# Phases and their trigonometry for two steps at a time in an S4 + SwiGLU block

## The chip, the cores and the metric

The kernel runs on one core of one Trainium2 chip. The core has a matrix engine (TensorE, PE), a vector engine (VectorE, DVE), an activation engine (ScalarE, ACT) and a general engine (GpSimd, POOL). Each works through its own list of instructions in order and waits on semaphores for what the others make. Loads and stores go through queues: most are issued by SyncE (SP), some by ACT and POOL. Weights and tables lie in the on-chip memory SBUF; PE writes its results to a small memory, PSUM, which DVE and ACT read. The metric is the device time of one execution in microseconds (us); less is better. The figure compared is the median of three executions.

## The reference, cut to what matters

```python
x = A_u                                              # (1, L=2048, D=640)
sa, ca, ga, sb, cb, gb = six rows of silu(c) @ w_mod
h = layernorm(x) * (1 + ca) + sa
x = x + ga * S4(h)
h = layernorm(x) * (1 + cb) + sb
x = x + gb * ((silu(h @ w1) * (h @ w3)) @ w2)        # F = 1728
# S4, for every channel d with N = 128 states n:
dt = exp(log_dt); logdA = dt * (A_re + i A_im); dB = dt * (B_re + i B_im)
K[d, l] = Re sum_n C[d, n] * dB[d, n] * exp(logdA[d, n] * l)      # l = 0 .. 2047
y = causal convolution of u with K over l (by FFT of length 2L) + u * Dskip
```

What matters here is K. For every channel and state the kernel needs exp of a real exponent times the cosine and sine of a phase, for 2048 values of l. It splits l = 64 a + b (a of 32, b of 64), so a channel needs only 32 + 64 complex factors per state, and the sum over the states becomes a matrix product of the "a" factors with the "b" factors.

## The kernel before, in words

The 640 channels are worked through in 40 **steps** of 16 channels (SD = 16); 8 steps are one chunk of 128 channels (SPC = 8). The states lie on the 128 partitions. A step s goes through these parts, each a short function with a two-letter name:

- PH (`phases`, lines 477-483, POOL): the phase in 32-bit integers, where a full turn is 2^32 and wraps by itself. One multiply of 16 channels x 64 factors (`thi` times the table `iota`), and one add of `phi` for the 32 "a" factors.
- AB, CO, SI (`absph`, `cosine`, `sine`, lines 485-496, ACT): the absolute value of the phase, from it the cosine, and the sine in place.
- PA, PQ (`exponents`, lines 441-454, PE): the real exponents, as a product of the transposed parameters `lx` with a selection table (`r2` for the 64 "b" factors, `r1` for the 32 "a" factors); each is two matmuls over all 128 rows, of 512 and of 256 columns. XA, XQ (`fast`, `slow`, ACT): exp of them, into the table A.
- E1, E2, A1, A2 (lines 504-518, DVE): exp times cosine into E, exp times sine in place into A. All four read both inputs from SBUF.
- kg (`kgen`, PE): 64 small products that give K of the step; K (`k1evac`, DVE, lines 537 and 538); pt (`k_stage1`, PE, line 548) and uk (`k_out`, ACT): the first stage of the transform of K.

A second group of parts does the convolution of an earlier chunk in 40 units of its own: st (`stage2`, PE, line 579, with the load of its table s2 on SP), kc (`k_copy`, ACT, a copy of half the result to SBUF), T (`products`, DVE, 596 and 597), Y (`sums`, DVE, 603 and 604), iv (`inverse1`, PE, 621, with its load of i1) and zt (`z_store`, ACT and a store).

From step 10 on, the parts follow an order written out by hand, the string `ROUND` (lines 829-835): one **round** takes four steps and four convolution units, and is repeated ten times (the first and last only in part). "E1+2" is part E1 of step 4*round + 2. In the rounds PE, ACT, DVE and POOL keep exactly this order (`keep_in_program_order`). Convolution units run with a lag of ten steps. Rounds 2 to 6 carry four extra pieces (LS, LP, LC, LO) that finish the modulation rows. The exponents of all steps share one pair of PSUM banks, so PA, XA, PQ, XQ of a step and PA of the next form a chain; st, kc, T, Y and the next st share another pair in the same way.

Before the rounds a prologue loads parameters, makes `lx` (`polar`, lines 232-292: the transposes of the tile `lt` at 282, a copy on ACT and a subtraction on DVE), the tables `r2` and `r1` (743, 747), the first layer norm and the transform of u. There a scheduler of the language sets the order. Behind the rounds come the last convolution units and then the SwiGLU part (all helper-recorded, so its lines read L103), which the change does not touch.

Lines that the prediction names: phases are lines 481 and 482 on POOL; AB, CO and SI are L136 `cs<-ph`, `cs<-cs` and `ph<-ph`, the exps L136 `A<-pa`; the copies kc, uk and zt are L139; E1, E2, A1, A2 are 506, 509, 513, 517.

## Time and profile before

| | us |
|---|---|
| median of 3 executions (997.47, 1000.23, 1000.56) | 1000.23 |
| the profiled execution, its own time | 991.63 |
| its span, first to last instruction | 989.8 |
| prologue, until the rounds are full (0 to 149) | 149 |
| full rounds (149 to 349) | 200 |
| last round, last convolution units (349 to 404) | 55 |
| SwiGLU part (404 to 990) | 586 |

How to read the profile: an answer of the timeline has a start, a duration, the engine, the line and the operation, then what it writes `<-` what it reads; in square brackets stands how long the engine had been idle and what released it. "xN" merges N instructions. Durations of neighbours on one engine overlap a little, since the next instruction starts while the last drains; the distance from start to start is then the cost, and the prediction calls it the cadence. A view by stretches gives the busy time of each engine within a piece of the span; the granted clock is the share of full speed that PE was allowed. A row of a group has the number of instructions, then their busy time and the mean of one in ns.

### The profile page before, as it was taken

The page shows a single profiled execution, that of the slowest core. Times are in us where ns is not written, and L with a number is a line of the kernel's source. Part 1 is how long each engine was busy: PE and PEld are TensorE (multiplying, and loading weights), DVE is VectorE, ACT ScalarE, POOL GpSimd, SP SyncE. Part 2 cuts the span into 40 slices and gives each one's busy share as a digit, 9 for nine tenths or more (in the row PEclk, how much of TensorE's full clock was granted, in tenths as well). Part 3 has the DMA queues.
Part 4 walks back from the last instruction along what each step waited for, and adds up shares of the span by engine and source line. Part 5 has one row for each costly group of instructions (what it writes and reads, how often), then busy time and mean ns, then how long its engine had stood idle before and what let it go on. Part 6 is the DMA issues. An engine that isn't in the chain of part 4 may idle for free.

```text
span 989.8 us, 20130 instructions
## 1 busy us (share of the span) xinstructions
PE 904.1 (91%) x7964; PEld 679.0 (69%) x7964; DVE 734.0 (74%) x1224; ACT 539.9 (55%) x792; POOL 348.5 (35%) x330
## 2 busy tenths in 40 slices
PE   5777779999999889789999999989899999999998
PEld 3334456666666666567888887676678888888786
DVE  5888978998888876677566675777696666676765
ACT  4759688899999943355333333453653333333332
POOL 1733344444444600323222232355342222314441
PEclk9865779999999999999999999999999999999999
DMA  9572285666676679691211104978231111123351
GB/s 265 206 253 93 108 196 140 174 180 175 195 220 152 176 199 291 201 246 53 67 54 54 54 28 140 256 221 261 80 120 54 54 55 57 56 87 94 96 205 72
DMA packets 103570, 140.72 MB, mean 142 GB/s; under 512 B 20564, under 2 KB 62676, under 8 KB 103476
## 3 DMA queue, kind: packets, MB, share of 16 engines
q1 hardware_dynamic: 92692, 113.60, 39.7%
q10 hardware_dynamic: 8480, 18.09, 6.2%
q0 software_dynamic: 2304, 7.74, 2.3%
q8 instruction: 63, 1.03, 0.4%
q14 instruction: 31, 0.25, 0.1%
HBM read 107.94 MB, written 31.46 MB: 141 GB/s over the span
## 4 chain that ended last, share of the span: by engine, by line
PE 42%; DVE 5%; DMA 3%; ACT 2%; POOL 2%; issue 2%; SPq 1%; DVEq 0%; ACTq 0%; POOLq 0%
PE ps L103 42%; DMA A<-zs 2%; DVE ul L103 1%; DVE T L103 1%; DVE xm L103 1%; DMA rw<-in_w_dram 1%; DVE gl L103 1%; ACT s L103 1%; ACT gh L103 1%; DMA xm<-in_x_dram 1%; SPq L103 1%; DVE s L103 1%; POOL s L103 0%; POOL S L103 0%; DVE h L103 0%
## 5 line engine op out<-in xcount | busy, mean ns | idle before, releaser
L103 DVE TENSOR_TENSOR s<-ps,s 128x512 f32<-128x512 f32 x138 | 94.6, 686 | 76.6 <-PE ps L103 76.0
L481 POOL TENSOR_TENSOR ph<-thi,iota 128x1024 int32<-128x1024 int32 x40 | 85.3, 2133 | 161.5 <-DVE A L517 101.1
L103 DVE TENSOR_TENSOR gl<-rw,gh 128x640 fp32r<-128x640 f32 x87 | 84.6, 972 | 62.6 <-ACT gh L103 62.5
L103 ACT CAST gh<-rw 128x640 fp32r<-128x640 f32 x87 | 63.2, 726 | 115.2 <-PE ps L103 77.2
L103 POOL TENSOR_TENSOR rw<-rw,gbr 128x512 f32<-128x512 f32 x56 | 82.2, 1476 | 105.0 <-DMA rw<-in_w_dram 87.2
L103 POOL TENSOR_TENSOR S<-rw 128x256 f32<-128x256 f32 x46 | 35.0, 764 | 176.4 <-DVE S0l L103 157.4
L579 PE MATMUL p<-uk,s 128*64 128x256 f32 x640 | 79.2, 390 | 15.8 <-PE pa L447 5.8
L103 PE MATMUL ps<-gh,uh 128*128 128x512 f32 x224 | 89.3, 398 | 0.0
L103 PE MATMUL ps<-gl,uh 128*128 128x512 f32 x224 | 89.2, 398 | 0.0
L103 PE MATMUL ps<-xA,gh 128*128 128x512 f32 x280 | 87.8, 392 | 0.7 <-ACT xA L103 0.4
L103 PE MATMUL ps<-gh,ul 128*128 128x512 f32 x208 | 82.7, 398 | 0.0
L136 ACT ACTIVATE A<-pa 128x1024 f32<-128x1024 f32 (+1 forms) x80 | 64.3, 813 | 27.1 <-PE pa L447 25.0
L579 PEld LDWEIGHTS p<-uk,s 128*64 128x64 f32 x640 | 45.9, 138 | 39.5 <-PE pa L447 8.4
L447 PE MATMUL pa<-r,lx 128*128 128x512 f32 (+1 forms) x160 | 52.1, 415 | 10.7 <-ACT A L136 5.6
L103 PEld LDWEIGHTS ps<-xA,gh 128*128 128x128 f32 x280 | 52.2, 188 | 13.7 <-ACT xA L103 1.0
L103 PE MATMUL ps<-xA,gl 128*128 128x512 f32 x140 | 54.6, 390 | 0.2 <-DVE gl L103 0.2
L513 DVE TENSOR_TENSOR A<-A,ph 128x1024 f32<-128x1024 f32 x40 | 52.6, 1315 | 0.0
L506 DVE TENSOR_TENSOR E<-A,cs 128x1024 f32<-128x1024 f32 x40 | 50.2, 1254 | 0.7 <-ACT cs L136 0.7
L103 PEld LDWEIGHTS ps<-gl,uh 128*128 128x128 f32 x224 | 43.1, 193 | 9.4
L447 PEld LDWEIGHTS pa<-r,lx 128*128 128x128 f32 x160 | 25.8, 203 | 34.5 <-ACT A L136 18.2
L103 PEld LDWEIGHTS ps<-gh,uh 128*128 128x128 f32 x224 | 43.2, 193 | 9.1
L530 PE MATMUL pk<-E 128*32 128x64 f32 x1280 | 46.4, 236 | 3.4 <-DVE E L509 3.4
(229 smaller groups left out, 2280.2 us busy)
## 6 DMA issues: line engine op xcount, KB each, us to landing
rw<-in_w_dram ACTq DMA_DIRECT2D x44, 320.0 KB
us<-u SPq DMA_DIRECT2D x16, 640.0 KB
s<-in_s_dram SPq DMA_DIRECT2D x40, 256.0 KB
i<-in_i_dram SPq DMA_DIRECT2D x40, 256.0 KB
rw<-in_wg_dram SPq DMA_DIRECT2D x31, 320.0 KB
rw<-in_wu_dram SPq DMA_DIRECT2D x28, 320.0 KB
uk<-us SPq DMA_DIRECT2D x32, 256.0 KB
zs<-zt SPq DMA_DIRECT2D x32, 256.0 KB
```

The source lines that it names most:

```text
L103: ins = fn(*args, **kw)
L136: return tc.keep_in_program_order(S.activation(*args, **kw))
L447: keep(PE.matmul(ps[:, rr, :8 * n], lx[:, s // SPC, 2 * (s % 2) + rr, :], table[:, js, :].rearrange("p j b -> p (j b)"), start=True, stop= ...
L481: hold(G.tensor_tensor(p, bc(thi[:, sl], 2, NPH), bc(iota, 1, SD), op=OP.mult))
L506: keep(V.tensor_tensor(EC[s][:, :, 1:3, :], AA[s][:, :, 1:3, :], mid(cs[s]), op=OP.mult))
L513: keep(V.tensor_tensor(A[:, :, 1:3, :], A[:, :, 1:3, :], mid(ph[s]), op=OP.mult))
L530: keep(PE.matmul(pk[dq * 32:dq * 32 + 32, g, :], x[:, g * 4 + dq, 1, :], x[:, g * 4 + dq, 0:3:2, :], start=(st == 0), stop=(st == 1), tile ...
L579: keep(PE.matmul(p2[par * 64:par * 64 + 64, pi, c, :], s2[:, pi * 2 + par, c * 64:c * 64 + 64], uk[:, 0:kn + 1:kn, f, :], start=True, stop ...
```

## The change

It takes the phases, AB, CO and SI for two steps in one instruction each (tiles of 32 channels instead of 16), builds the 32 "a" phases differently, reads the exponents from 32 rows instead of 128, and puts the parts of a round in a new order.

- **Phases.** Only 8 of the 32 "a" phases are multiplied out and given `phi`; the other 24 are these 8 plus one of three multiples of 1024 times the step's `thi`. Per two steps: one multiply of 32 x 43, one add of 32 x 8, one add of 32 x 24. The "a" axis is rolled by 8, so that these 8 stand last; the constants follow.
- **AB, CO, SI** run on 128 x 2048 for even steps only. The tile `ph` has three buffers of two steps (four of one before), `cs` two of two steps (three of one before).
- **Exponents.** `lx` is arranged so that each group of 8 channels has its 32 rows (8 channels, two parameters, a high and a low part); a matmul names its 32 rows and its place in the array. The two matmuls of a part use neighbouring groups of 32 rows. `r2` shrinks from 2048 to 512 columns, `r1` from 1024 to 256. `lt` is made per pair of chunks, with every value written twice, and its transposes are 4 of 128 columns instead of 8 of 64.
- **Buffers.** K1, s2 and i1 have two buffers instead of three; the tile `part` is gone, other places serve for it.
- **ROUND** is new. CO and SI now stand once for two steps, AB and PH too.

The order that results on DVE around the start of a round, first before: `E_` is the product with the cosine, `T_`/`p2_` are the two halves of T, `Y_` are the sums, `pk_`/`K1_` are K; the row `E_2265` is E1 of the round's first step.

```order
L604 TENSOR_TENSOR Y_2217<-T_2201,p2_2134 128x2x128
L506 TENSOR_TENSOR E_2221<-A_1996,cs_2027 128x16x64
L509 TENSOR_TENSOR E_2221<-A_1996,cs_2027 128x16x32
L513 TENSOR_TENSOR A_1996<-A_1996,ph_1868 128x16x64
L517 SCALAR_TENSOR_TENSOR A_1996<-ph_1868,A_1996 128x16x32
L506 TENSOR_TENSOR E_2265<-A_2042,cs_2092 128x16x64
L596 TENSOR_TENSOR T_2282<-p2_2226,kc_2267 128x512
L597 TENSOR_TENSOR p2_2226<-p2_2226,kc_2267 128x4x128
```

and in the change, where `E_2583` is that E1:

```order
L527 SCALAR_TENSOR_TENSOR A_2323<-ph_2082,A_2323 128x16x32
L606 TENSOR_TENSOR T_2537<-p2_2468,kc_2481 128x512
L607 TENSOR_TENSOR p2_2468<-p2_2468,kc_2481 128x4x128
L547 TENSOR_TENSOR pk_2494<-pk_2494,dz_76 128x4
L548 TENSOR_TENSOR K1_2552<-pk_2494,gaT_75 128x256
L613 TENSOR_TENSOR Y_2555<-T_2537,p2_2468 128x2x128
L614 TENSOR_TENSOR Y_2555<-T_2537,p2_2468 128x2x128
L516 TENSOR_TENSOR E_2583<-A_2401,cs_2403 128x16x64
L523 TENSOR_TENSOR A_2401<-A_2401,ph_2319 128x16x64
L606 TENSOR_TENSOR T_2632<-p2_2560,kc_2629 128x512
L607 TENSOR_TENSOR p2_2560<-p2_2560,kc_2629 128x4x128
```

Between the sums Y of one unit and the products T of the next there stood E1, E2, A1, A2 and E1; now there stand E1 and A1 only, and E1, E2, A1, A2 are spread over the round.

ACT, from the load of the Sin table to the copy of the next round's first unit, before (`cs_` and `ph_` are the phases of one step):

```order
L136 ACT_TABLE_LOAD
L136 ACTIVATE cs_2027<-cs_2027 128x1024
L139 COPY kc_2195<-p2_2134 128x512
L136 ACTIVATE cs_2092<-cs_2092 128x1024
L139 COPY zt_2213<-pz_2108 128x2x4x128
L139 COPY uk_81<-pt_2204 128x32x16
L136 ACTIVATE ph_1868<-ph_1868 128x1024
L136 ACTIVATE cs_2119<-cs_2119 128x1024
L136 ACTIVATE ph_1957<-ph_1957 128x1024
L136 ACTIVATE cs_2250<-ph_2148 128x1024
L139 COPY kc_2267<-p2_2226 128x512
L136 ACTIVATE cs_2250<-cs_2250 128x1024
```

and in the change:

```order
L141 ACT_TABLE_LOAD
L141 ACTIVATE ph_2319<-ph_2319 128x32x64
L144 COPY kc_2481<-p2_2468 128x512
L141 ACTIVATE cs_2403<-cs_2403 128x2048
L144 COPY uk_81<-pt_2528 128x32x16
L141 ACTIVATE cs_2579<-ph_2485 128x2048
L141 ACTIVATE cs_2579<-cs_2579 128x2048
L144 COPY kc_2629<-p2_2560 128x512
L141 ACTIVATE ph_2485<-ph_2485 128x32x64
L144 COPY uk_81<-pt_2585 128x32x16
L141 ACT_TABLE_LOAD
```

The copies kc now stand behind one or two instructions of 2048 columns where they stood behind one of 1024; the number of table loads in a round stays two.

POOL, two steps of phases before:

```order
L481 TENSOR_TENSOR ph_1737<-thi_91,iota_74 128x1024
L482 TENSOR_TENSOR ph_1737<-ph_1737,phi_92 128x16x32
L481 TENSOR_TENSOR ph_1868<-thi_91,iota_74 128x1024
L482 TENSOR_TENSOR ph_1868<-ph_1868,phi_92 128x16x32
L481 TENSOR_TENSOR ph_1957<-thi_91,iota_74 128x1024
```

and in the change:

```order
L488 TENSOR_TENSOR ph_1918<-ph_1918,phi_92 128x32x8
L489 TENSOR_TENSOR ph_1918<-ph_1918 128x32x24
L487 TENSOR_TENSOR ph_2082<-thi_91,iota_74 128x32x43
L488 TENSOR_TENSOR ph_2082<-ph_2082,phi_92 128x32x8
L489 TENSOR_TENSOR ph_2082<-ph_2082 128x32x24
```

Three instructions now make two steps, where four did; nothing else stands on POOL in the rounds.

The diff, cut to its core:

```diff
@@ consts
+    slow = np.roll(np.arange(NA), -8)
+    s1 = s1[:, slow].reshape(P, 2, P)
+    iota = np.concatenate([-(128 * slow[-8:] + 63), 2 * np.arange(NA) + 1, -1024 * np.arange(1, NG)])
...
@@ polar
         for k in range(0, nk, 2):
             n = min(2, nk - k)
+            lt = pm_.tile([P, 2, 16, 2, 2, 8], F32, name="lt")
+            two = lambda v: bc(nat(v)[:, k + i], 2, 2)
+            for i in range(n):
+                E.tensor_tensor(lt[:, i, :, :, 0], two(are), two(dtc), op=OP.mult)
+            for i in range(n):
+                V.tensor_tensor(lt[:, i, :, :, 1], two(q), two(ld), op=OP.add)
...
-            acopy(to, pT[:, :n])
-            V.tensor_tensor(to[low], pT[low, :n], to[low].bitcast(F32), op=OP.subtract)
+            act(to, pT[:, :n], AF.Copy, scale=lo_sign)
+            V.scalar_tensor_tensor(to, pT[:, :n], is_lo, to.bitcast(F32), op0=OP.mult, op1=OP.add)
@@ exponents
-                keep(PE.matmul(ps[:, rr, :8 * n], lx[:, s // SPC, 2 * (s % 2) + rr, :],
-                               table[:, js, :].rearrange("p j b -> p (j b)"), start=True, stop=True))
+                q = (2 * (s % 2) + rr) * NA
+                rows = slice(q, q + NA)
+                keep(PE.matmul(ps[:, rr, :8 * n], lx[rows, s // SPC, s % SPC // 2, :],
+                               table[rows].rearrange("p j b -> p (j b)"), start=True, stop=True, tile_position=(q, 0)))
@@ phases, absph, cosine, sine
-        p = tp.tile([P, SD, NPH], I32, name="ph", bufs=4)
+        p = tp.tile([P, 2 * SD, NPG], I32, name="ph", bufs=3)
...
-        hold(G.tensor_tensor(p, bc(thi[:, sl], 2, NPH), bc(iota, 1, SD), op=OP.mult))
-        keep(G.tensor_tensor(p[:, :, :NA], p[:, :, :NA], bc(phi[:, sl], 2, NA), op=OP.add))
-        ph[s] = p
+        hold(G.tensor_tensor(p[:, :, b0:], bc(thi[:, sl], 2, NPG - b0), bc(iota, 1, 2 * SD), op=OP.mult))
+        keep(G.tensor_tensor(base, base, bc(phi[:, sl], 2, 8), op=OP.add))
+        keep(G.tensor_tensor(p[:, :, :b0].rearrange("p k (g j) -> p k g j", j=8), bc(base, 2, NG - 1),
+                             bc(p[:, :, NPH:], 3, 8), op=OP.add))
+        ph[s] = p[:, :, :NPH]
...
-        c = tp.tile([P, SD, NPH], F32, name="cs", bufs=3)
-        act(c, ph[s], AF.Abs)
+        cs[s] = tp.tile([P, 2 * SD, NPH], F32, name="cs")
+        act(cs[s], ph[s], AF.Abs)
...
-        dst = tp.tile([P, SD // 4, NB], F32, name="K1", bufs=3)
+        dst = tp.tile([P, SD // 4, NB], F32, name="K1")
...
-        s2 = fp.tile([P, 4, P], F32, name="s2", bufs=3)
+        s2 = fp.tile([P, 4, P], F32, name="s2")
...
-        i1 = fp.tile([P, 2, 2, P], F32, name="i1", bufs=3)
+        i1 = fp.tile([P, 2, 2, P], F32, name="i1")
@@ prologue
-    V.tensor_tensor(r2, bc(selx, 2, NB), bc(stepx[:, :NB], 1, NA), op=OP.mult)
+    V.tensor_tensor(r2, bc(selx, 2, NB), bc(stepx[:, :NB], 1, 8), op=OP.mult)
...
-    V.tensor_tensor(r1, bc(selx, 2, NA), bc(stepx[:, NB:], 1, NA), op=OP.mult)
+    V.tensor_tensor(r1, bc(selx, 2, NA), bc(stepx[:, NB:], 1, 8), op=OP.mult)
...
-    do("PH", 1)
     do("PH", 2)
...
-        do("PH", tk + 3)
+        do("PH", tk + 4)
@@ ROUND
-        "E1+2 kc+2 pt+0 CO+4 PH+5 T+2 kg+1 SI+3 PA+4 K+1 SI+4 Y+2 uk+0 E2+2 st+3 E1+3 XA+4 A1+2 kc+3 "
-        "PQ+4 A2+2 pt+1 XQ+4 T+3 PH+6 PA+5 kg+2 XA+5 Y+3 uk+1 K+2 PQ+5 st+4 A1+3 XQ+5 zt+1 E1+4 AB+5 "
-        "PA+6 E2+3 pt+2 XA+6 A2+3 E2+4 kc+4 PQ+6 uk+2 PH+7 T+4 kg+3 XQ+6 AB+6 LS+4 PA+7 K+3 iv+2 XA+7 "
-        "AB+7 LP+4 Y+4 PQ+7 A1+4 LC+4 st+5 XQ+7 LO+4 A2+4 PH+8 kg+4 CO+5 iv+3 kc+5 K+4 CO+6 T+5 pt+3 "
-        "zt+3 Y+5 uk+3 E1+5 SI+5 st+6 CO+7 E2+5 A1+5 SI+6 iv+4 AB+8 A2+5 iv+5 "
+        "E1+2 pt+0 CO+4 kg+1 A1+2 kc+2 SI+4 T+2 PA+4 uk+0 XA+4 Y+2 E2+2 st+3 K+1 zt+1 kc+3 A2+2 kg+2 "
+        "PQ+4 XQ+4 pt+1 E1+3 uk+1 PA+5 PH+6 XA+5 E2+3 K+2 pt+2 A1+3 E1+4 A2+3 T+3 PQ+5 uk+2 Y+3 XQ+5 "
+        "iv+2 PA+6 A1+4 kg+3 XA+6 AB+6 PQ+6 XQ+6 st+4 PA+7 K+3 iv+3 kc+4 XA+7 E1+5 PQ+7 zt+3 T+4 LS+4 "
+        "Y+4 XQ+7 SI+6 E2+4 LP+4 A2+4 st+5 kc+5 CO+6 E2+5 PH+8 LC+4 A1+5 LO+4 kg+4 A2+5 pt+3 T+5 uk+3 "
+        "iv+4 K+4 Y+5 st+6 iv+5 AB+8 "
```

More of the change, by code (lines that the diff above doesn't have):

```diff
@@ L64, in consts @@
     i2 = np.concatenate([np.cos(ang).T, -np.sin(ang).T] * 2)
-    iota = np.zeros((P, NPH), np.int32)
-    iota[:, :NA] = -(128 * np.arange(NA) + 63)
-    iota[:, NA:] = 2 * np.arange(NA) + 1
-    selx = np.tile(np.eye(NA), (4, 1))
-    stepx = np.tile(np.concatenate([np.arange(NB), 64.0 * np.arange(NA)]), (4, NA, 1)).reshape(P, NB + NA)
-    stepx[P // 4:P // 2] = stepx[3 * P // 4:] = np.repeat((0, 0.5), (NB, NA))
+    slow = np.roll(np.arange(NA), -8)
+    s1 = s1[:, slow].reshape(P, 2, P)
+    iota = np.concatenate([-(128 * slow[-8:] + 63), 2 * np.arange(NA) + 1, -1024 * np.arange(1, NG)])
+    iota = np.tile(iota.astype(np.int32), (P, 1))
+    row = np.arange(P)
+    selx = row[:, None] % 8 == np.arange(8)
+    of_m = row[:, None] // 8 % 2 == 1
+    stepx = np.where(of_m, np.repeat((0, 0.5), (NB, NA)), np.concatenate([np.arange(NB), 64.0 * slow]))
+    is_lo = (row // 16 % 2)[:, None]
     c1 = s1r.reshape(4, NA, 2 * NA).sum(axis=1, keepdims=True).repeat(NA, axis=1).reshape(P, 2 * NA)
@@ L180, in tile_kernel @@
     cols = pm_.tile([P, 7, KD], F32, name="cols")
[L181 to L185 removed]
+    widths = (8, NB + NA, 2 * NA, 2 * NA, 1, P, NA, 1, 1)
+    misc = pm_.tile([P, sum(widths)], F32, name="misc")
+    selx, stepx, s1r, c1, one4m, toq, tog, is_lo, lo_sign = (
+        misc[:, sum(widths[:i]):sum(widths[:i + 1])] for i in range(len(widths)))
     tiny = pm_.tile([P, 1], F32, name="tiny")
@@ L768, in tile_kernel @@
     ln1_norm(2)
-    for n in ("AB", "CO", "SI"):
-        do(n, 1)
     for i, t in enumerate(("pb", "pk", "pb")):
```

63 lines of the change are left out of this document (29 added, 34 removed).

## The prediction

> **What bounds it now.** First the stretches and the chain of waits, to see where the change can act.
>
> ```profile
> core 0: us, PE busy (x) PEld busy (x) DVE busy (x) ACT busy (x) POOL busy (x), PEclk, DMA share, GB/s
> 0.00:118.00 118.00, 86.11 (x943) 47.15 (x945) 93.52 (x197) 75.64 (x95) 45.35 (x46) 0.74 0.56 188
> 149.00:349.00 200.00, 183.04 (x3334) 131.14 (x3329) 175.86 (x294) 181.28 (x223) 92.41 (x65) 1.00 0.66 178
> ...
> 453.15 142.01 PE ps L103 x625
> ```
>
> The columns after each stretch are its length and the busy time of each engine. From 404 us on the SwiGLU part runs, which the change does not touch; its long pieces in the chain are PE alone (142 us without a break), so a gain made earlier is kept. In the full rounds no engine is the plain bound: of 200 us PE is busy 183.0, ACT 181.3, DVE 175.9. Three engines at about nine tenths, each in a fixed order, are bound by who waits for whom, so I read DVE's timeline through a round:
>
> ```profile
> 146.43 2.67 DVE L506 TENSOR_TENSOR E<-A,cs 128x1024 f32<-128x1024 f32 x1
> ...
> 177.49 1.22 DVE L506 TENSOR_TENSOR E<-A,cs 128x1024 f32<-128x1024 f32 x1
> ...
> 206.23 1.22 DVE L506 TENSOR_TENSOR E<-A,cs 128x1024 f32<-128x1024 f32 x1
> ...
> 224.75 0.42 DVE L603 TENSOR_TENSOR Y<-T,p 128x256 f32<-128x256 f32 x1 [1.21 <-PE pz L621]
> ...
> 228.77 0.17 DVE L537 TENSOR_TENSOR pk<-pk,dz 128x4 f32<-128x4 f32 x1 [1.47 <-PE pk L530]
> 228.97 0.42 DVE L538 TENSOR_TENSOR K<-pk,gaT 128x256 f32<-128x256 f32 x1
> 229.32 0.68 DVE L596 TENSOR_TENSOR T<-p,kc 128x512 f32<-128x512 f32 x1
> ...
> 230.83 0.42 DVE L603 TENSOR_TENSOR Y<-T,p 128x256 f32<-128x256 f32 x1
> ...
> 231.50 1.22 DVE L506 TENSOR_TENSOR E<-A,cs 128x1024 f32<-128x1024 f32 x1
> 232.64 0.68 DVE L509 TENSOR_TENSOR E<-A,cs 128x512 f32<-128x512 f32 x1
> 233.24 1.22 DVE L513 TENSOR_TENSOR A<-A,ph 128x1024 f32<-128x1024 f32 x1
> 234.37 0.68 DVE L517 SCALAR_TENSOR_TENSOR A<-ph,A 128x512 f32<-128x512 f32 x1
> 234.98 1.22 DVE L506 TENSOR_TENSOR E<-A,cs 128x1024 f32<-128x1024 f32 x1
> ...
> 320.53 1.22 DVE L506 TENSOR_TENSOR E<-A,cs 128x1024 f32<-128x1024 f32 x1
> ...
> 348.38 1.22 DVE L506 TENSOR_TENSOR E<-A,cs 128x1024 f32<-128x1024 f32 x1
> ```
>
> The rows of L506 that open a round are 206.23 and 234.98: 28.75 us a round in rounds 2 to 6 (round 2, 146.43 to 177.49, took 31.06), and 320.53 to 348.38, 27.85, in rounds 7 and 8, which lack the four extra pieces. Cadences, start to start: K 0.55, T 1.51, Y 0.67, E1 1.14, E2 0.60, A1 1.13, A2 0.61, together 6.21 us a step, 24.8 for four; the extra pieces cost up to 0.9 (28.75 - 27.85), I take 0.7. So DVE has 25.5 us of work in a round of 28.75 and waits 3.2: 1.21 for iv and 1.47 for kg in the two bracketed rows, the rest in small ones.
>
> **ACT.**
>
> ```profile
> 214.91 1.02 ACT L136 ACTIVATE A<-pa 128x1024 f32<-128x1024 f32 x1 [1.09 <-PE pa L447]
> ...
> 223.65 1.02 ACT L136 ACTIVATE A<-pa 128x1024 f32<-128x1024 f32 x1 [1.16 <-PE pa L447]
> ...
> 234.20 1.04 ACT L136 ACTIVATE cs<-ph 128x1024 f32<-128x1024 int32 x1
> 235.15 0.57 ACT L139 COPY kc<-p 128x512 f32<-128x512 f32 x1
> 235.61 1.07 ACT L136 ACTIVATE cs<-cs 128x1024 f32<-128x1024 f32 x1
> ...
> L139 ACT COPY zt<-pz 128x1024 f32<-128x1024 f32 x16 | 16.2, 1010 | 1.9 <-DMA zs<-zt 1.3 <-PE pz L621 0.5
> ...
> L139 ACT COPY uk<-pt 128x512 f32<-128x512 f32 x40 | 23.4, 584 | 1.7 <-PE pt L548 1.6
> ```
>
> AB takes 0.95 from start to start (234.20 to 235.15). From 512 to 1024 columns a copy grows from 584 to 1010 ns, so 1024 columns more cost 0.85: two steps in one take 0.95 + 0.85 = 1.80 instead of 1.90. Six such pairs a round save 0.6 us of ACT's 26.1 (181.3 x 28.75 / 200). The 1.09 and 1.16 in brackets are waits for the exponents' matmuls. The price of the longer instruction is that a copy kc behind it waits up to 0.85 longer.
>
> **PE.**
>
> ```profile
> 207.82 0.32 PE L530 MATMUL pk<-E 128*32 128x64 f32 x8
> ...
> 208.85 0.73 PE L447 MATMUL pa<-r,lx 128*128 128x512 f32 x2
> ...
> 231.69 1.95 PE L579 MATMUL p<-uk,s 128*64 128x256 f32 x16 [0.86 <-PE pt L548]
> ...
> 241.43 0.51 PE L447 MATMUL pa<-r,lx 128*128 128x256 f32 x2 [0.36 <-ACT A L136]
> ...
> L447 PE MATMUL pa<-r,lx 128*128 128x512 f32 x80 | 30.9, 477 | 3.3 <-DVE u L433 3.2
> ...
> L427 PE MATMUL pu<-x,misc 32*64 32x320 f32 x256 | 31.3, 675 | 12.9 <-ACT u L139 6.7 <-ACT x L136 3.6 <-DVE u L433 2.6
> ```
>
> Two matmuls of PA take 0.73, of PQ 0.51. No row shows this product on 32 rows. The bounds: if the two run one after the other as now, nothing changes; if they run side by side, one of each pair is saved. In the group of L447 the 80 matmuls of 477 ns add to 38 us within 30.9 busy, hardly overlapped; in L427, which uses groups of 32 rows (and two of columns), 256 of 675 ns add to 173 within 31.3, five or six at once. I take the second: 0.25 + 0.15 a step, 1.6 us a round of PE's 26.3 (183.0 x 28.75 / 200). That is what lets PE stay ahead of DVE.
>
> **POOL, and its port.**
>
> ```profile
> L481 POOL TENSOR_TENSOR ph<-thi,iota x40: 1899/1906/2820, 15.5 to 334.9; 128x1024 int32<-128x1024 int32 x40
> L482 POOL TENSOR_TENSOR ph<-ph,phi x40: 1038/1046/1976, 19.0 to 337.2; 128x512 int32<-128x512 int32 x40
> ...
> 146.12 1.90 POOL L481 TENSOR_TENSOR ph<-thi,iota 128x1024 int32<-128x1024 int32 x1 [1.83 <-DVE pk L537]
> 148.10 1.91 POOL L482 TENSOR_TENSOR ph<-ph,phi 128x512 int32<-128x512 int32 x1
> ...
> 235.20 2.75 POOL L481 TENSOR_TENSOR ph<-thi,iota 128x1024 int32<-128x1024 int32 x1 [4.72 <-DVE A L517]
> ...
> 216.52 1.49 DVE L513 TENSOR_TENSOR A<-A,ph 128x1024 f32<-128x1024 f32 x1
> ```
>
> Minima of 1899 ns for 1024 columns and 1038 for 512 give 1.68 ns a column and 0.18 fixed, if multiply and add cost alike. Two steps cost 2 x 2.94 = 5.9 us now; the new three cost 2.5 (1376 columns), 0.6 (256) and 1.5 (768), 4.6. POOL is idle half the round, so the saving itself is worth nothing. What counts is when it runs. At 146.12 POOL's multiply was under way when E1 came (146.43): E1 took 2.67 instead of 1.22, and the add at 148.10 took 1.91 instead of 1.04; at 235.20 POOL came second, behind E1 of 234.98, and took 2.75. So E1, E2, A1, A2 and POOL exclude each other, and the first keeps the other out until it is done; T, K and Y beside POOL keep their times (229.32 to 231.50 in the fence above, while POOL worked). In rounds 3 to 8 the eight POOL instructions of a round fall so that only one row stands longer, A1 at 216.52 by 0.3.
>
> **The new round, walked by hand with these cadences.** Time 0 is DVE's E1+2, right behind Y+5. That Y frees the PSUM pair of st, so st+6 takes 1.95 from there and kc 0.58 behind it: with handoffs kc is done at 2.7, or at 3.3 if ACT is still in CO+4. DVE has only E1 and A1 to put there and is free at 2.27, so T+2 waits 0.4 to 1.1; I take 0.7, and T+2 runs to 4.5, Y+2 to 5.15. E2, K+1, A2, E1+3 and E2+3 fill the time to 8.6. Meanwhile PE does st+3 (from 5.2) and kg+2 (1.03, to 8.2), so K+2 finds it. A1+3, E1+4, A2+3 lead to T+3 at 12.0, whose kc was done at 9; Y+3 ends at 14.2, and st+4 behind it at 16.2, kc+4 at 17.0. DVE reaches T+4 at 17.4 after A1+4, K+3, E1+5: no wait, but a narrow one. Y+4 ends at 19.6, st+5 at 21.6; ACT by then has XQ+7, a table load and SI+6 behind it and gives kc+5 at 23.0. DVE reaches T+5 at 23.9 with E2, the late piece, A2, E2, A1, A2, and Y+5 ends at 26.7.
>
> In this walk the port is counted as 0.5: PH+6 waits for the last A2 of the round before, and its multiply (2.5) fits under T+5, K+4 and Y+5 (2.7); PH+8 starts behind A2+3, its multiply runs under T+3 and Y+3 (2.2) and holds A1+4 for 0.3; the short adds 0.2. Loads: with two buffers, s2 is asked for when the st two before it ends, which is at least 4 us ahead of its use here, and stands on SP behind a store of zt at most; 0. K1 with two buffers is read one part before it is rewritten; 0. Handoffs that I can't see: 0.3. The round: 25.5 of work + 0.7 + 0.5 + 0.3 = 27.0, and 26.3 in rounds 7 and 8. Below, the bound is 25.5 and 0.5; above, what the rivals say.
>
> **The ends.**
>
> ```profile
> 8.88 2.28 DVE L743 TENSOR_TENSOR r<-misc 128x2048 fp32r<-128x2048 f32 x1
> ...
> 13.23 1.21 DVE L747 TENSOR_TENSOR r<-misc 128x1024 fp32r<-128x1024 f32 x1
> ```
>
> `r2` and `r1` shrink to a quarter: 2.28 + 1.21 becomes about 0.9, 2.6 us less on DVE; the doubled `lt` gives back 0.9 (six of its ten writes are DVE's, 128 columns more each, 1.2 ns a column by E1's 1.22 us for 1024). The prologue is 118 us with DVE busy 93.5, and waits for loads and for PE at a clock of 0.74, so I count half, 1 us. The first phases come 1.6 later (4.6 against 2.9) and the first cosines are two steps long; both lie under the exponents of steps 0 to 3, and bound what could be lost at 3 us. Behind the rounds nothing changes.
>
> **Sum.** Rounds 2 to 6: 5 x 1.75 = 8.75; rounds 7 and 8: 2 x 1.55 = 3.1; prologue 1. Together 12.9 us: the profiled execution would go from 991.63 to 979, and the median, 8.6 us above it, from 1000.23 to **987.5**. Its own range is 981 to 994.
>
> **Rivals.**
>
> *PE gains nothing.* If the 32-row matmuls run one after the other, PE keeps 26.3 us of work, and in its order it also waits (st+2 for Y, PQ for XA, PA for XQ), 1.7 us if as little as two of the gaps of 0.8 remain: 28.0 a round, 7 x 0.75 = 5, about 995. The same time comes out if ACT's long instructions hold kc twice a round for 0.85. For it: no row has this form. Against: L427.
>
> *POOL takes the port first* (the slower one). The multiply of PH+6 has 0.2 us to spare under T+5, K+4, Y+5. If A2+5 slips behind T+5's wait, or the add comes before E1+2, then E1+2 or A1+2 stands for a multiply or for the long add, and the same at A1+4 and E1+5. It decides from 2.25 us of such waits a round (1.75 and the 0.5 already counted). A multiply and a short add, 3.1 a round, give 29.6: 7 x 0.85 = 6 us lost, about 1005. For it: the row 146.43 lost 1.45 in this way. Against: the row 216.52, 0.3 a round for eight POOL instructions.
> The Trainium skill's page "SBUF — State Buffer" (section "Who interferes with whom") states this as a rule: a VectorE instruction with two SBUF inputs and a GpSimd instruction that reads SBUF exclude each other, and whoever issues first keeps the pair for the whole instruction. The rows at 146.43 and 235.20 agree, 2.67 and 2.75 us. By that rule alone fewer but longer POOL instructions are the worse neighbours, which speaks against this change.
>
> *Everything fits.* No port waits, T+2's gap filled by a faster ACT: 25.5 + 0.5 = 26.0, 7 x 2.7 = 19, with 3 in the prologue: 978.
>
> *The merged instructions don't do what they say*: if 2048 columns cost twice 1024 and the order merely shifts the waits, no change, 1000.
>
> **Chances.** Forecast 0.5; everything fits 0.12; PE gains nothing 0.2; port 0.13; no change 0.05. About 0.3% (3 us) is what a measurement of this kernel tells from no change. Faster: 0.5 + 0.12 + 0.15 of the 0.2 = 0.77; same: the other 0.05, the 0.05 and a little of the port, 0.12; slower 0.11. The range 975 to 1002 leaves out the far ends of the port and of the good case, one tenth each.
>
> **What would show it.** Right: rows that open a round 27.0 apart; pairs of L447's successor starting together; AB at 1.9; POOL at 2.5, 0.6, 1.5; E1 at 1.2. Wrong: E1 or A1 of 2 us and more beside POOL; PE without gaps at 28; T waiting over 1.1 for kc; s2 among the releasers of PE.

## The result, and the profile after

Over 20 runs of each, the kernel before has a median of 999.4 us and the changed one 992.2 us. The ratio, estimated over all runs (the quotient of the two medians is 0.9927), is 0.9932, with a 95% interval of 0.9917 to 0.9948, which is 6.8 us less, or 5.2 to 8.3. Beside two groups of the experiments the changed kernel was timed again and came out at 0.9940 (0.9919 to 0.9961) and 0.9932 (0.9908 to 0.9955) of the kernel before. So the change makes the kernel faster, as forecast, but by 6.8 us where the forecast had 12.7.

The stretch of the rounds in the changed kernel, which answers to the one shown of before (length, then busy us of PE, PEld, DVE, ACT, POOL):

```profile
149.00:349.00 200.00, 182.51 (x3382) 129.29 (x3384) 186.42 (x297) 185.29 (x187) 89.42 (x48) 0.96 0.66 184
```

In the rounds PE has 182.5 us of 200, DVE 186.4, ACT 185.3: still three engines at nine tenths. VectorE's rows that open a round (L506 before, L516 now), with the wait for kc that follows in the first full round:

```profile
156.66 3.27 DVE L516 TENSOR_TENSOR E<-A,cs 128x1024 f32<-128x1024 f32 x1
...
187.65 1.29 DVE L516 TENSOR_TENSOR E<-A,cs 128x1024 f32<-128x1024 f32 x1
189.05 1.48 DVE L523 TENSOR_TENSOR A<-A,ph 128x1024 f32<-128x1024 f32 x1
191.60 0.69 DVE L606 TENSOR_TENSOR T<-p,kc 128x512 f32<-128x512 f32 x1 [1.07 <-ACT kc L144]
...
202.74 1.69 DVE L523 TENSOR_TENSOR A<-A,ph 128x1024 f32<-128x1024 f32 x1
...
214.73 1.29 DVE L516 TENSOR_TENSOR E<-A,cs 128x1024 f32<-128x1024 f32 x1
...
241.80 1.29 DVE L516 TENSOR_TENSOR E<-A,cs 128x1024 f32<-128x1024 f32 x1
...
269.55 1.29 DVE L516 TENSOR_TENSOR E<-A,cs 128x1024 f32<-128x1024 f32 x1
...
297.91 1.29 DVE L516 TENSOR_TENSOR E<-A,cs 128x1024 f32<-128x1024 f32 x1
...
324.95 1.23 DVE L516 TENSOR_TENSOR E<-A,cs 128x1024 f32<-128x1024 f32 x1
326.29 2.43 DVE L523 TENSOR_TENSOR A<-A,ph 128x1024 f32<-128x1024 f32 x1
...
352.03 1.22 DVE L516 TENSOR_TENSOR E<-A,cs 128x1024 f32<-128x1024 f32 x1
```

Rounds 3 and 4 take 27.08 and 27.07 us (28.74 and 28.75 before), rounds 5 and 6 here 27.75 and 28.36, rounds 7 and 8 27.04 and 27.08. In rounds 3 and 4 E1 lasts 1.29, A1+2 1.48 and A1+4 1.69 beside POOL, where all three last 1.22 alone, and T+2 waits 1.07 for kc.

This execution took 1000.3 us, the longest of its 20, and the profiled one of before 991.6, shorter than all of its 20. So two single profiles can't be subtracted; the differences below are read from stretches that agree between executions. With the further profiles that the experiments gave of both kernels (times in us; "first u" is the start of the first VectorE copy of the u tile, "last pz" the end of the last inverse matmul):

| profile | first u | round 2 starts | round 2 | rounds 3 to 6 | rounds 7, 8 | round 9 to last pz | span |
|---|---|---|---|---|---|---|---|
| before | 33.48 | 146.43 | 31.06 | 28.74, 28.75, 28.85, 28.84 | 27.86, 27.85 | 52.1 | 989.8 |
| before, 2nd | 39.26 | 149.99 | 32.72 | 28.74, 28.74, 28.84, 28.84 | 27.87, 27.86 | 51.2 | 998.8 |
| changed | 42.91 | 156.66 | 30.99 | 27.08, 27.07, 27.75, 28.36 | 27.04, 27.08 | 54.5 | 998.5 |
| changed, 2nd | 40.29 | 151.08 | 30.52 | 27.08, 27.36, 27.53, 27.99 | 26.65, 27.17 | 53.0 | 991.3 |
| changed, 3rd | 38.79 | 150.19 | 30.94 | 27.07, 27.08, 27.40, 27.22 | 26.63, 27.17 | 53.3 | 989.9 |

From round 2 to round 9 the means are 202.8 and 194.4, 8.4 us less; from there to the last pz 51.6 and 53.6, 2.0 us more. The sum, -6.4, is the measured -6.8 within its interval. What varies between executions of one kernel lies for the most part ahead of round 2, and behind the last pz.

The three edits as single instructions. TensorE's exponents, by shape (busy, mean ns):

```profile
L451 PE MATMUL pa<-r,lx 32*128 32x512 f32 x80 | 23.6, 583 | 2.4 <-DVE u L436 1.7 <-ACT A L141 0.5
L451 PE MATMUL pa<-r,lx 32*128 32x256 f32 x80 | 17.1, 423 | 3.1 <-ACT A L141 2.2
```

and ScalarE, TensorE and GpSimd around the opening of round 4:

```profile
214.29 1.93 ACT L141 ACTIVATE cs<-ph 128x2048 f32<-128x2048 int32 x1
216.25 1.92 ACT L141 ACTIVATE cs<-cs 128x2048 f32<-128x2048 f32 x1
218.07 0.56 ACT L144 COPY kc<-p 128x512 f32<-128x512 f32 x1
...
214.92 1.95 PE L589 MATMUL p<-uk,s 128*64 128x256 f32 x16 [0.45 <-ACT uk L144]
...
219.94 0.50 PE L451 MATMUL pa<-r,lx 32*128 32x512 f32 x2
...
13.58 2.50 POOL L487 TENSOR_TENSOR ph<-thi,iota 128x1376 int32<-128x1376 int32 x1 [13.14 <-DVE thi L270]
17.70 0.64 POOL L488 TENSOR_TENSOR ph<-ph,phi 128x256 int32<-128x256 int32 x1 [1.62 <-DVE phi L295]
18.42 1.58 POOL L489 TENSOR_TENSOR ph<-ph 128x768 int32<-128x768 int32 x1
...
215.02 1.50 POOL L488 TENSOR_TENSOR ph<-ph,phi 128x256 int32<-128x256 int32 x1
216.60 2.46 POOL L489 TENSOR_TENSOR ph<-ph 128x768 int32<-128x768 int32 x1
```

Two matmuls of 512 columns now take 0.50 (0.73 before), and the 80 of each shape have 23.6 and 17.1 us busy where they had 30.9 and 21.3. The merged cosine takes 1.82 from start to start (216.25 to 218.07). GpSimd alone needs 2.50, 0.64 and 1.58, as forecast (the rows at 13 to 18 us, where VectorE leaves it alone); in the rounds its short add takes 1.50 and its long one 2.46, since E1 and A1 hold the port. And the reason for T+2's wait is in these rows: the second stage's matmuls (214.92, 1.95) end at 216.87, but kc starts at 218.07, behind the two-step CO+4 on ScalarE.

### The profile page after: what moved, and what is told of

The parts are those of the page before. It is cut to its first block, busy times and chain, and to the rows that moved or that the text cites. A ratio compares the mean times of both kernels' runs of the same rounds, so it can differ in the third digit from the quotient of the medians.

```text
span 998.5 us, 19955 instructions
## 1 busy us (share of the span) xinstructions
PE 911.9 (91%) x7924; PEld 681.0 (68%) x7924; DVE 737.4 (74%) x1224; ACT 535.6 (54%) x732; POOL 340.6 (34%) x310
## 4 chain that ended last, share of the span: by engine, by line
PE 43%; DVE 4%; DMA 3%; ACT 2%; issue 2%; POOL 1%; SPq 0%; DVEq 0%; ACTq 0%; POOLq 0%
PE ps L108 43%; DMA A<-zs 1%; DMA xm<-in_x_dram 1%; DVE ul L108 1%; DVE T L108 1%; DVE xm L108 1%; ACT s L108 1%; ACT gh L108 1%; DVE s L108 1%; SPq L108 0%; DMA rw<-in_w_dram 0%; DVE gl L108 0%; POOL s L108 0%; POOL S L108 0%; ACT T L108 0%
## 5 line engine op out<-in xcount | busy, mean ns | idle before, releaser
L108 POOL TENSOR_TENSOR rw<-rw,gbr 128x512 f32<-128x512 f32 x56 | 84.5, 1515 | 106.0 <-DMA rw<-in_w_dram 87.7
L589 PE MATMUL p<-uk,s 128*64 128x256 f32 x640 | 82.3, 401 | 16.3 <-DMA s<-in_s_dram 7.1
L487 POOL TENSOR_TENSOR ph<-thi,iota 128x1376 int32<-128x1376 int32 x20 | 51.0, 2552 | 128.5 <-DVE A L527 94.7
L558 PE MATMUL pt<-s,K 128*64 128x128 f32 x640 | 52.9, 306 | 4.6 <-ACT uk L144 4.6
L523 DVE TENSOR_TENSOR A<-A,ph 128x1024 f32<-128x1024 f32 x40 | 55.6, 1391 | 0.9
L516 DVE TENSOR_TENSOR E<-A,cs 128x1024 f32<-128x1024 f32 x40 | 51.2, 1281 | 0.3 <-ACT cs L141 0.3
L558 PEld LDWEIGHTS pt<-s,K 128*64 128x64 f32 x640 | 40.7, 152 | 13.7 <-ACT uk L144 7.6
```

The costliest lines, as they stand in the source:

```text
L108: ins = fn(*args, **kw)
L487: hold(G.tensor_tensor(p[:, :, b0:], bc(thi[:, sl], 2, NPG - b0), bc(iota, 1, 2 * SD), op=OP.mult))
L516: keep(V.tensor_tensor(EC[s][:, :, 1:3, :], AA[s][:, :, 1:3, :], mid(cs[s]), op=OP.mult))
L523: keep(V.tensor_tensor(A[:, :, 1:3, :], A[:, :, 1:3, :], mid(ph[s]), op=OP.mult))
L558: keep(PE.matmul(pt[c * 64:c * 64 + 64, g, :], kk[:, g, :], s1[:, c, :], start=True, stop=True, tile_position=(0, c * 64)))
L589: keep(PE.matmul(p2[par * 64:par * 64 + 64, pi, c, :], s2[:, pi * 2 + par, c * 64:c * 64 + 64], uk[:, 0:kn + 1:kn, f, :], start=True, stop ...
```

## The experiments

### Both matmuls of a pair on one group of rows

```
-                q = (2 * (s % 2) + rr) * NA
+                q = 2 * (s % 2) * NA
```

> The changed kernel with both matmuls of a pair on the same group of 32 rows, so that they can't run side by side (the second one's exponents are then those of the first one's rows: that part of the output is wrong, the amount of work is the same). Theory: side by side saves TensorE 0.25 and 0.15 a step, 1.6 us a round, and that is what lets TensorE stay ahead; without it T+2 waits for kc and K+2 for kg by more, rounds go from 27.1 to 27.8, and the time rises by 5 to 8 us, to about 998. Rival: TensorE has that much to spare in the new order, and the gain comes from the order and ScalarE: within 1.5 us of 992.2.

Measured: 1004.36 us, 1.0077 (1.0047 to 1.0106) of the kernel before; round 2 took 32.3, rounds 3 to 8 27.4 to 28.2. The groups of this kernel:

```profile
L451 PE MATMUL pa<-r,lx 32*128 32x512 f32 x80 | 32.8, 513 | 2.3 <-DVE u L436 1.3 <-ACT A L141 0.9
L451 PE MATMUL pa<-r,lx 32*128 32x256 f32 x80 | 22.1, 370 | 1.5 <-ACT A L141 0.6
```

The theory holds in the rounds. The busy time rises from 23.6 to 32.8 and from 17.1 to 22.1 us: 0.23 and 0.13 us a step, 1.4 a round, so two groups of 32 rows do run side by side. Of these 1.4 a round VectorE sees 0.8 (27.83 against 27.08 in round 3). From round 2 to round 9 it is 5.1 us more than in the changed kernel. The time rose by more than that (12 us against the run with three buffers for s2 on the same chip); 6 us of that, by the two profiles, lie ahead of round 2, which starts at 157.81 instead of 151.68. Eight matmuls of 256 columns near the start took 1.08 us in this kernel's profile and 0.64 in the other's, so TensorE's speed there (see the section on the start) is likely a part of it; how much is not shown.

### Exponents on 32 rows alone, and the old order with all the new parts

The first is the kernel before with only the tables, the transposed inputs and the matmuls of the exponents changed; the second is the changed kernel with the order of before:

```
     ROUND = (
-        "E1+2 pt+0 CO+4 kg+1 A1+2 kc+2 SI+4 T+2 ...
+        "E1+2 kc+2 pt+0 CO+4 PH+5 T+2 kg+1 SI+3 ...
```

> The kernel before, with only the exponents on 32 rows (the tables r1, r2 and the transposed inputs with them). Theory: TensorE's work falls by 1.6 us a round, of which VectorE's wait for kg (1.47) gives back perhaps half: rounds of 28.1, and with a microsecond from the smaller tables about 994. Rival: no change in the rounds, since the wait is for the order and not for TensorE's speed: 28.7 a round, 998 to 999. In the first 45 us the trace shows also whether TensorE's matmuls are slow there (1.0 us for eight of the 256 columns instead of 0.64) because of the new tables, or only in the one execution that was profiled.

> The changed kernel with the order of the parts of a round as it was before (the two-step parts stand at the place of the even step). Theory: the new parts by themselves save little, since VectorE's waits for iv and kg in the old order (1.2 and 1.5 us a round) come from the order; rounds of 28.2 and 27.5, about 999 less 7 x 0.5 = 996, so over half of the gain is the order's. Rival: the shorter work of TensorE and ScalarE takes these waits away in the old order too: 992 or less.

Measured: 32 rows alone 999.35 us, 1.0026 (0.9999 to 1.0053): no gain; rounds 3 and 4 fell from 28.74 to 28.43, and round 8 rose to 29.5. The rival was nearer. The old order with the new parts: 1027.01 us, 1.0315 (1.0289 to 1.0341). Both its theory and its rival were wrong by far: rounds 3 to 5 took 31 us, rounds 6 to 8 28.8 to 33.6. VectorE in its round 4, from 217.55 to 248.49, and then TensorE ahead of the first of these rows:

```profile
223.06 0.17 DVE L547 TENSOR_TENSOR pk<-pk,dz 128x4 f32<-128x4 f32 x1 [2.13 <-PE pk L540]
...
238.63 1.88 DVE L523 TENSOR_TENSOR A<-A,ph 128x1024 f32<-128x1024 f32 x1
...
242.28 0.17 DVE L547 TENSOR_TENSOR pk<-pk,dz 128x4 f32<-128x4 f32 x1 [1.11 <-PE pk L540]
```

```profile
215.37 3.48 PE L589 MATMUL p<-uk,s 128*64 128x256 f32 x16 [1.97 <-ACT uk L144]
```

K waits 2.13 and 1.11 us for the matmuls of kg, and A1 stands 1.88 beside POOL. Ahead of the longer wait the second stage had itself waited 1.97 for a copy uk, which in this order stands behind a two-step cosine and a zt on ScalarE. This run has the two-step parts at one place of the old order, that of the even step; another place was not tried.

### One step at a time in the new order

Each word of the order that stands for two steps now issues two one-step instructions; phases are 1024 columns of multiply and 512 of add a step again.

```
             do(name, k)
+            if name in by_two:
+                do(name, k + 1)
```

> The changed kernel with phases, Abs, cosine and sine one step at a time as before (each word of the new order that stood for two steps now issues the two one behind the other; in the start of the program they come as before, exponents on 32 rows stay). Theory: two steps at a time are worth 0.6 us of ScalarE's and 1.3 of GpSimd's time a round, of which VectorE sees part: rounds of 27.8 instead of 27.1, while round 2 starts 4 to 5 us earlier, in sum within 2 us of the changed kernel. Rival: the new order was made for the merged instructions (as the old order lost 20 us with them) and falls apart without them: rounds of 29 or more, 10 us slower or worse.

Measured: 1014.22 us, 1.0146 (1.0106 to 1.0186); rounds of 30.2 to 30.6 (29.3 the last). Here the rival was right. VectorE in its round 3, from 187.28 to 217.82:

```profile
187.28 1.82 DVE L510 TENSOR_TENSOR E<-A,cs 128x1024 f32<-128x1024 f32 x1
...
195.34 2.39 DVE L513 TENSOR_TENSOR E<-A,cs 128x512 f32<-128x512 f32 x1
...
198.18 1.53 DVE L517 TENSOR_TENSOR A<-A,ph 128x1024 f32<-128x1024 f32 x1
...
205.16 1.53 DVE L510 TENSOR_TENSOR E<-A,cs 128x1024 f32<-128x1024 f32 x1
...
211.00 2.92 DVE L517 TENSOR_TENSOR A<-A,ph 128x1024 f32<-128x1024 f32 x1
...
213.92 1.46 DVE L521 SCALAR_TENSOR_TENSOR A<-ph,A 128x512 f32<-128x512 f32 x1
```

Against 1.22 for E1 and A1 and 0.68 for E2 and A2 these six last 5.4 us longer in a round, beside POOL, where the changed kernel loses 0.07, 0.26 and 0.47. In this round no instruction of VectorE waits for another engine's result, so 5.4 less 0.8, less the 1.07 of T+2's wait, is the 3.5 us by which it is longer than the changed kernel's (30.54 against 27.08). So what the two-step parts are worth here is on the port far more than on ScalarE. I read it so: 5.9 us of POOL for two steps no longer fit under the T, K and Y that this order puts together, 4.6 us nearly do; the run changed ScalarE's instructions with them, so the split is by these rows alone. Together with the two runs above: the new order without the two-step parts loses 14 us, the new parts in the old order lose 31, and the exponents on 32 rows by themselves gain nothing.

### The wait for kc filled, and taken away

Both kernels are the one of the section on the start below, with the order changed in one place:

```
 filled:      ... A1+2 kc+2 E2+2 SI+4 T+2 ... A1+3 K+2 ...
 taken away:  E1+2 pt+0 kc+2 CO+4 kg+1 A1+2 SI+4 T+2 ...
```

> The kernel of the run with the start by single steps, with E2+2 put ahead of T+2 and K+2 behind A1+3 in the order of a round. Theory: T+2 waits 1.1 us for kc while VectorE has nothing to do; E2+2 (0.6) fills that, so rounds fall from 27.1 to 26.5, and the time by 3 to 4 us against that run. Rival: what follows is set by TensorE (the second stage, then the matmuls of kg), so VectorE only waits later, at K+2 or T+3: rounds stay at 27.1.

> The kernel of the run with the start by single steps, with kc+2 put ahead of CO+4 in the order of a round. Theory: kc+2 stands on ScalarE behind the two-step CO+4 (1.91 us) and starts 1.2 us after the second stage's result is there; ahead of it T+2's wait of 1.07 goes, and rounds fall from 27.1 to 26.1, 7 us in all against that run, so about 982. Rival: ScalarE then idles 0.6 us ahead of kc and is itself late later on (kc+5 holds T+5), or POOL's long add, which now runs in T+2's wait, moves under E2+2: rounds of 26.8 or more.

Measured: filled 994.89 us, 0.9970 (0.9943 to 0.9998), rounds of 27.7 to 28.3; taken away 992.29 us, 0.9941 (0.9916 to 0.9966), rounds of 27.6 to 28.0. In neither is any of rounds 3 to 8 as short as the same one of the changed kernel at its best, and from round 2 to round 9 they take 198.4 and 197.1 us, where the kernel with the same start and the order unchanged takes 192.6. Both theories fell; the rival of the second, rounds of 26.8 or more, held, and the first came out longer than its rival had it. First VectorE of the filled one, then of the other:

```profile
180.81 2.08 DVE L519 TENSOR_TENSOR E<-A,cs 128x512 f32<-128x512 f32 x1
...
197.13 0.69 DVE L606 TENSOR_TENSOR T<-p,kc 128x512 f32<-128x512 f32 x1 [0.45 <-ACT kc L144]
```

```profile
182.16 0.69 DVE L606 TENSOR_TENSOR T<-p,kc 128x512 f32<-128x512 f32 x1
...
190.50 1.23 DVE L516 TENSOR_TENSOR E<-A,cs 128x1024 f32<-128x1024 f32 x1 [0.74 <-ACT A L141]
...
198.14 0.69 DVE L606 TENSOR_TENSOR T<-p,kc 128x512 f32<-128x512 f32 x1 [0.41 <-ACT kc L144]
```

E2+2 (L519), put into the gap, took 2.08 instead of 0.68: the gap was where POOL's long add ran (from 179.88 here). T+4 (197.13) now waits 0.45 for its kc as well. With kc ahead of the cosine T+2 no longer waits (it starts 2.8 us into the round, 182.16 behind 179.36, instead of 3.95), but E1+4 waits 0.74 for ScalarE's table A, and T+4 0.41 for its kc. So the wait of 1.07 was no slack that could be had: GpSimd's port time and ScalarE's order stand behind it.

### Three buffers for s2

```
-        s2 = fp.tile([P, 4, P], F32, name="s2")
+        s2 = fp.tile([P, 4, P], F32, name="s2", bufs=3)
...
-        T = fp.tile([P, 2, 2, DC], F32, name="T")
+        T = fp.tile([P, 2, 2, DC], F32, name="T", bufs=1)
```

> The changed kernel with three buffers for s2 again (T, which only VectorE writes and reads, gives up its second one to make room). Theory: with two buffers the load of s2 is late where the second stage runs every 3 us, behind the rounds; TensorE waits there 2.7 and 1.9 us for it in the changed kernel's trace, and the prediction had put this at 0. With three buffers these waits go, and the time falls from 992.2 by 3 to 5 us, to about 988; the rounds stay at 27.1. Rival: that stretch is set by the stores of zs and by the copies of ScalarE, and the wait only moves: within 1 us of 992.2.

> The changed kernel, beside the next run on the same chip, as its measure: 0.993 to 0.995 of the kernel before, rounds 3 and 4 at 27.1, and TensorE's waits for s2 behind the rounds (2.2 to 2.7 and 1.4 to 1.9 us) as in its two profiles.

> The changed kernel with three buffers for s2 again, as in the first run with it, now beside the changed kernel itself. Theory (the waits for s2 are on the path): its profiles had 192.7 us from round 2 to round 9 instead of 194.3 and 195.4, and the last inverse matmuls 0.6 to 2.1 us earlier behind that; 2 to 4 us faster than the changed kernel, a ratio to it of 0.996 to 0.998. Rival: what the traces gain is lost in the part behind the rounds, as the first timing of it (0.9962 of the kernel before, against 0.9932 and 0.994 for the changed kernel on other chips) would have it: no difference or slower.

Measured: first 992.26 us, 0.9962 (0.9944 to 0.9981) of the kernel before; then, beside the changed kernel (991.29 us, 0.9932), 993.87 us, 0.9948 (0.9927 to 0.9970). TensorE's waits of 140 to 420 us, of the changed kernel in the first and third profile (what waited, for what: us in total, times, longest):

```profile
PE p L589 <- DMA s<-in_s_dram: 7.1, 4, 2.7
```

```profile
PE p L589 <- DMA s<-in_s_dram: 3.9, 3, 3.0
```

With three buffers no such row is left, and the time is the same: the theory fell. In the third profile the two waits behind the rounds are 3.0 and 0.6, not the 2.2 to 2.7 and 1.4 to 1.9 expected. Of waits of 7.1, 6.2 and 3.9 us in the three profiles of the changed kernel little reaches the end: from round 2 to round 9 it took 195.4, 194.3 and 193.5 us, with three buffers 192.8 and 193.3, and from there to the last pz 54.5, 53.0 and 53.3 against 52.4 and 53.5. The traces show a part of the reason why it doesn't reach the end. `i1`, the table of the inverse, was also cut from three buffers to two, and with s2 early TensorE waits for i1 instead, 3.0 us behind the rounds in the first profile with three buffers:

```profile
381.14 1.16 PE L631 MATMUL pz<-Y,i 64*128 64x128 f32 x16 [2.31 <-DMA i<-in_i_dram]
```

In the kernel before TensorE waits there for neither table. A run with three buffers for both tables was not made. So the prediction's 0 for s2 alone was right within what the times can tell, though s2 does stand among TensorE's releasers, which it had named as a sign of being wrong.

### The start of the program

The changed kernel and the kernel before once more, for their profiles, and the changed kernel (with three buffers for s2) with the first phases, Abs, cosines and sines by halves of a two-step tile, in the sequence of before:

```
+    def halves(name, k, n):
+        h, m = slice(k % 2 * SD, k % 2 * SD + n * SD), k - k % 2
...
+            ks = [j for j in ((k, k + 1) if in_order[0] else (k,)) if (name, j) not in done and 0 <= j < NS]
...
-        do("PH", tk + 4)
+        do("PH", tk + 3)
```

> The changed kernel itself once more, beside the three below on one chip, for a second profile of it. Theory (the rounds gain 6 to 7 us, the start of the program loses 4 to 5 by the two-step parts): rounds 3 and 4 again at 27.1, round 2 starting at 150 to 152 us where TensorE speeds up at 17 us (eight matmuls of 256 columns in 0.64 us), at 156 to 158 where it stays slow (1.08) until 40 us. Rival: the late start of 156.7 belongs to the one profiled execution, and round 2 starts at 146 to 147 as before.

> The changed kernel with three buffers for s2 (and one for T), and the phases, Abs, cosine and sine of the program's start done in halves of their two-step tiles, one step at a time in the sequence of the kernel before; from the rounds on two steps at a time. Theory: the two-step parts cost 4 to 5 us in the start (the first cosines wait for a phase of two steps and last twice as long, and the copies and modulation sums queue behind), so round 2 starts at 147 or, with a slow TensorE, at 152; with the 4 us of s2 the time is 984, 8 us below the changed kernel. Rival: the late start comes from the exponents on 32 rows or from TensorE's clock alone: round 2 at 151 or 157 as in the changed kernel, and 988.

> The kernel before once more, for a second profile of it; its first one (991.6) was faster than all executions that were timed. Theory (the changed kernel's start costs nothing by itself, and the early first u of 33.5 us belongs to that one execution): first u at 38 to 42 us and round 2 at 150 to 154, as in the profiles with the changed start. Rival: the exponents on 32 rows delay the start: first u at 33 to 35 and round 2 at 146 to 148 again.

Measured: the changed kernel 992.94 us (0.9940); by halves 989.08 us, 0.9914 (0.9880 to 0.9948), first u at 41.17 and round 2 at 153.58; the kernel before, in one execution, 1000.64 us. My theory of that point, that the two-step parts cost 4 to 5 us in the start, fell; the last of the three runs came out as its theory had it, first u at 39.26 and round 2 at 149.99, so the first profile of before had a lucky start. From the first u to round 2 it is 113.0 and 110.7 us before, 113.8, 110.8 and 111.4 in the changed kernel, 112.4 by halves. Most of what differs comes ahead of the first u, and there the executions of one kernel differ by TensorE's speed. Before and its second profile, then the changed kernel:

```profile
20.41 0.64 PE L300 MATMUL pm<-A,sc 128*32 128x256 f32 x8
...
27.55 1.30 PE L324 MATMUL pr<-ident,cols 128*64 128x128 f32 x10 [2.01 <-DVE cols L320]
```

```profile
21.64 1.08 PE L300 MATMUL pm<-A,sc 128*32 128x256 f32 x8
...
31.40 2.40 PE L324 MATMUL pr<-ident,cols 128*64 128x128 f32 x10 [1.32 <-DVE cols L320]
```

```profile
24.16 1.08 PE L303 MATMUL pm<-A,sc 128*32 128x256 f32 x8
...
34.81 2.39 PE L327 MATMUL pr<-ident,cols 128*64 128x128 f32 x10 [2.51 <-DVE cols L323]
...
20.00:30.00 10.00, 9.49 (x48) 4.48 (x48) 2.95 (x9) 2.22 (x3) 0.00 (x1) 1.00 0.91 269
```

Eight matmuls of 256 columns take 0.64 or 1.08 us, ten of 128 take 1.30 or 2.39, in either kernel. A start that is by itself better or worse by a microsecond can't be told from this; a loss of 4 would not fit, since rounds and tail already give 6.4 of the 6.8 us measured. The two kernels of the section on the wait for kc also start by halves: their first u comes at 35.79 and 35.97 and their round 2 at 147.56 and 148.40, earlier than in any profile of the changed kernel. TensorE was fast sooner in these two executions (granted clock 0.82 and 0.89 from 30 to 40 us, against 0.50 in the third profile of the changed kernel), so what the halves give is not separated from that.

By halves is the fastest kernel that was timed, but its interval and the changed kernel's lie over one another, so it isn't shown to be faster.

## Why the prediction was right, and where it was half wrong

**What bounds it.** Right: no engine alone does, and the three at nine tenths are still there. The two runs on the wait for kc show it best: what is taken from one wait comes back at the next engine.

**ScalarE.** 1.80 was forecast for a merged instruction from start to start; 1.82 was measured where the next doesn't read its result (216.25 to 218.07), and 1.96 where it does (214.29 to 216.25), which the forecast hadn't in it: in a round the five merged instructions whose follower doesn't read their result save 0.08 each, the one that the next reads costs 0.06 more, and 0.3 of the 0.6 is left. The price named beside it, a kc that stands behind the long instruction, came due at T+2 in rounds 2 to 7.

**TensorE.** 0.25 and 0.15 a step were forecast from the rows of L427; 0.23 and 0.13 were measured. The rival in which the matmuls run one after the other is out, by the run that made them do so.

**GpSimd and its port.** 2.5, 0.6 and 1.5 were forecast, 2.50, 0.64 and 1.58 measured. The port was put at 0.5 a round and takes 0.8 by the durations (0.07, 0.26 and 0.47), of which the first two lie inside T+2's wait. The rival in which POOL takes the port first was not this kernel, but it was near: one step at a time, or E2+2 moved by a few places, brings it about. The Trainium skill's page "SBUF — State Buffer" (section "Who interferes with whom") gives the exclusion, and the rows agree (2.08 for E2, 2.43 for A1 at 326.29). By that rule alone, I had written, fewer and longer instructions are the worse neighbours; the run by single steps shows the opposite here, 5.4 us against 0.8, where the total is 5.9 instead of 4.6 us for two steps.

**The round.** 27.0 was forecast from 25.5 of work, 0.7 for T+2, 0.5 for the port and 0.3 of handoffs; rounds 3 and 4 took 27.07. The mechanism is there (T+2's wait for kc, the port, the work in the new order), but that the sum came out to a tenth is partly luck: T+2's wait was 0.4 larger than forecast, the port 0.3 larger, and what is left for work and handoffs is 25.2 where the forecast had 25.8. And it was multiplied too far:

- Rounds 3 to 6 were to gain 7.0 and gained 5.5 (sums of 115.2 before and 109.7 as a mean of three). Rounds 5 and 6 carry longer late pieces (a copy of 256 columns more on VectorE), which the old order had hidden in its waits: 27.4 and 27.1 in the profiles with three buffers for s2, and up to 27.8 and 28.4 where s2 is late as well (the first profile).
- Rounds 7 and 8 were to gain 3.1 and gained 1.8: 26.3 was forecast, 26.6 to 27.2 measured. The step that failed is kc+5, which the walk had done at 23.0, 0.9 ahead of VectorE. In the first profile it is done 24.5 into round 3 (the first row below, behind a two-step sine on ScalarE), just when VectorE comes. In rounds 7 and 8, which lack the late pieces, VectorE comes earlier and waits for it: 0.69 in round 7 of this profile (the second row), 0.3 in the other rounds 7 and 8. In round 8 T+4 waits 0.3 too.

```profile
211.55 0.57 ACT L144 COPY kc<-p 128x512 f32<-128x512 f32 x1
...
322.42 0.69 DVE L606 TENSOR_TENSOR T<-p,kc 128x512 f32<-128x512 f32 x1 [0.69 <-ACT kc L144]
```

- Round 2 was to gain 1.75 and gained 1.1; it starts with a POOL multiply under E1 (3.27 in the row at 156.66), as it did before (2.67), and its T+2 then waits 2.3 to 3.0 for kc in the three profiles, where that wait was 1.2 and 2.3 before.

**The ends.** The microsecond for the smaller tables can't be found: it is 0 within what the start varies. "Behind the rounds nothing changes" is the other step that failed: it is 2.0 us longer there. One cause that suggests itself is the new order: the row that opens a round is not the same point of the work in both, and in the last round T+2 comes 1.1 us behind it before (349.52 behind 348.38) and 2.8 now (354.86 behind 352.03). But this lag doesn't last. The fifth T of that stretch comes 22.5 us behind the opening in both kernels (before first):

```profile
349.52 0.68 DVE L596 TENSOR_TENSOR T<-p,kc 128x512 f32<-128x512 f32 x1
...
370.85 0.69 DVE L596 TENSOR_TENSOR T<-p,kc 128x512 f32<-128x512 f32 x1 [2.48 <-ACT kc L139]
```

```profile
354.86 0.69 DVE L606 TENSOR_TENSOR T<-p,kc 128x512 f32<-128x512 f32 x1 [0.28 <-ACT kc L144]
...
374.54 0.69 DVE L606 TENSOR_TENSOR T<-p,kc 128x512 f32<-128x512 f32 x1 [1.63 <-ACT kc L144]
```

And the two kernels of the section on the wait for kc have the same lag or more (T+2 at 2.8 and 3.1) and still take 52.0 and 52.1 from round 9 to the last pz, as before. So this lag is not the cause; what is lost comes after the fifth T. There TensorE waits for s2 in the changed kernel (4.7, 3.6 and 3.6 us in its three profiles) and, with three buffers for s2, for i1 (3.0 in one of them), and in the kernel before for neither. Late loads of s2 alone can be no more than a part, since the five profiles with three buffers for s2 have 52.0 to 53.5, between before (51.2 and 52.1) and the changed kernel (53.0 to 54.5). The smaller buffers for s2 and i1 together are a likely cause; the prediction had put the loads at 0 by a walk through a full round. No run has taken both back, so the cause stays open.

In sum: 11.85 was forecast for rounds 2 to 8 and 8.4 came, 1 for the start and 0 came, 0 behind and -2.0 came. That is 6.4 for 12.85 (which, off the median of 1000.23, is 987.4; the prediction has 987.5).

## What to carry to other kernels

Where three engines are each nine tenths busy in fixed orders, an order and the lengths of the pieces are one design: here the new order without the two-step parts loses 14 us, the new parts in the old order lose 31, and together they gain 7. A wait in such a kernel may be another engine's cover, so look at what runs in it (here GpSimd's add in VectorE's gap) before filling it. And a walk through one steady round should not be multiplied over rounds that lack a piece, nor taken to the ends: walk the last round and the tail too, or count only the steady ones. A buffer that a steady round doesn't need may be needed where the same part runs more often.
